# Attention's key-value products in four parts, one in front of each output tile of the last batch; query transposes gathered behind them

## The chip, the cores and the metric

The kernel runs on one core of a Trainium2 chip. The metric is device time in microseconds for one execution of the whole program. The engines are named as in the profile: PE (TensorE, matrix products and transposes), PEld (its weight loads), DVE (VectorE), ACT (ScalarE), POOL (GpSimd) and SP (SyncE, which issues DMAs).

## The reference, cut to what matters

Three stages follow each other: linear attention with a norm per head, a layer of eight experts with one chosen per token, and a gated layer. The change touches only the first.

```python
def _attn_ref(q, k, v, g_norm):          # 8 batches, 8 heads, 576 rows, 64 columns
    kv = np.einsum('bhsd,bhse->bhde', k, v)
    out = np.einsum('bhsd,bhde->bhse', q, kv)
    rms = np.sqrt(np.mean(out * out, axis=-1, keepdims=True) + 1e-06)
    return (out / rms * g_norm).astype(np.float32)
...
x = attn_out.transpose(0, 2, 1, 3).reshape(B * S, H * D)
x = _moe_ref(x=x, **moe_kwargs)          # logits, argmax, two products per expert
return _moe2_ref(x=x, **moe2_kwargs)     # (sigmoid(x @ w_gate) * (x @ w_val)) @ w_out
```

## The kernel before

The order of the instructions on each engine is the order in which the program emits them; no scheduler moves them. Each engine and each DMA queue works its own list in order and waits where an operand or a buffer isn't ready.

The attention stage is a loop over nine rounds, b = 0 to 8. Round b makes the key-value product of batch b and the outputs of batch b - 1. Inside, r runs from 0 to 4 over tiles of 128 query rows; the fifth tile of a pair of batches is shared, so only rounds with an even b make an output for r = 4, and only rounds with an odd b transpose a fifth query tile.

- emit_kv(b) does 72 products of 64x64 on PE (four pairs of heads c, nine row groups, two heads): the tile kv in PSUM. In the trace each fp32 product appears as two weight loads and two products, so 144 of each. Two DVE copies (L263, L264) put kv into R, block diagonal, in SBUF.
- emit_RT(b) transposes R on PE (L271, tile rtp), and DVE copies it to SBUF (L273). emit_M(b) multiplies it with the routing weights on PE (L279, tile mp), and DVE copies the 16 columns per pair back into R (L280).
- emit_qT transposes one query tile on PE (L285, tile qps); ACT copies it out (L287).
- emit_out(b - 1, r) is one output tile: products on PE (L299, tile ops), a copy and a square on ACT (L301, L304), a sum of squares on DVE (L305, into ssq).
- norm(b - 2), called at r = 1, is a chain of eight DVE operations (L314 to L328) with one ACT square root in it. rank (L349 to L368, even b from 4 on, at r = 1), lanes (L375, r = 3) and choose (odd b, r = 3) are routing steps, mostly on DVE.
- load_kv(b + 2) and load_q(b + 2) issue the loads on SP at r = 1. Keys and values have two buffers each, so the loads of batch b + 2 wait until emit_kv(b) has read its own.

In the kernel before, all of emit_kv(b) stands at the head of the round, and then each r has one output tile and one transpose of queries. PSUM has two buffers each for kv, rtp and mp together, for qps, and for ops.

Behind the attention comes a chain of small DVE steps that sort the tokens by expert, and then the two expert products and the gated layer, both long rows of matrix products.

Of the kernel before, what the change touches and what calls it, by code (L numbers as in the profile page):

```python
# [9 lines left out]
F32 = mybir.dt.float32  # L10
# [10 lines left out]
B, H, S, D = 8, 8, 576, 64  # L21
# [61 lines left out]
def attention_moe_glu_kernel(  # L83
# [4 lines left out]
    nc = tc.nc  # L88
# [70 lines left out]
    with ExitStack() as st:  # L159
# [3 lines left out]
        pkv = st.enter_context(tc.tile_pool(name="a_pkv", bufs=2, space=PSUM))  # L163
# [27 lines left out]
        Rs = [big.tile([128, 4, 144], F32, name=f"R{i}") for i in range(3)]  # L191

        q_t, k_t, v_t, qr_t = {}, {}, {}, {}

        def load_kv(b):

            if b < B:
                for src, dst, nm in ((k, k_t, "kt"), (v, v_t, "vt")):
                    t = dst[b] = ld.tile([128, 4, 9, D], F32, tag=nm, name=nm)
                    eng = nc.scalar if b == 0 and src is v else nc.sync  # L200
                    eng.dma_start(out=t.rearrange("p c r d -> p c (r d)"), in_=src[b].rearrange("(c i) (p r) d -> (i p) c (r d)", i=2, r=9))

        def load_q(b):

            if b < B:
                q_t[b] = ld.tile([128, H, 4, D], F32, tag="qt", name="qt")
                nc.sync.dma_start(out=q_t[b], in_=q[b, :, 0:512, :].rearrange("h (p r) d -> p h r d", r=4))
                if b % 2 == 0:
                    qr_t[b // 2] = ld.tile([128, H, D], F32, tag="qr", name="qr")
                half = slice(64 * (b % 2), 64 * (b % 2) + 64)  # L210
                nc.sync.dma_start(out=qr_t[b // 2][half], in_=q[b, :, 512:576, :].rearrange("h p d -> p h d"))
# [38 lines left out]
                    op=ALU.mult)  # L250
            nc.vector.tensor_tensor(out=bias, in0=bias, in1=lg, op=ALU.add)

        qT, o_t, me_t = {}, {}, {}

        def emit_kv(b):
            kv = pkv.tile([128, 4, 64], F32, tag="kv", name="kv")
            kt, vt, R = k_t.pop(b), v_t.pop(b), Rs[b % 3]
            for c in range(4):
                for r in range(9):
                    for i in range(2):  # L260
                        rows = slice(64 * i, 64 * i + 64)
                        nc.tensor.matmul(out=kv[rows, c, :], lhsT=kt[rows, c, r, :], rhs=vt[rows, c, r, :], start=(r == 0), stop=(r == 8))
            nc.vector.tensor_copy(out=R[0:64, :, 0:64], in_=kv[0:64])  # L263
            nc.vector.tensor_copy(out=R[64:128, :, 64:128], in_=kv[64:128])  # L264

# [9 lines left out]
        def emit_M(b):  # L275
            rt = mps_t.pop(b)
            ps = pkv.tile([128, 4, 128], F32, tag="kv", name="mp")
            for hp in range(4):
                nc.tensor.matmul(out=ps[:, hp, 0:16], lhsT=rt[:, hp, :], rhs=wpt[:, hp, :], start=True, stop=True)  # L279
            nc.vector.tensor_copy(out=Rs[b % 3][:, :, 128:144], in_=ps[:, :, 0:16])  # L280

        def emit_qT(key, src):
            ps = pq.tile([128, 4, 128], F32, tag="q", name="qps")
            for hp in range(4):
                nc.tensor.transpose(out=ps[:, hp, :], in_=src[:, hp * 128:hp * 128 + 128], identity=ident)  # L285
            t = wk.tile([128, 4, 128], F32, tag="qT", name="qT", bufs=5)
            nc.scalar.activation(out=t, in_=ps, func=ACTF.Copy)  # L287
            qT[key] = t
# [18 lines left out]
        def norm(b):  # L307

            r0, n = 4 * (b % 2), 4 + b % 2
            t0 = 9 * (b // 2) + r0  # L310
            rt, tt = (sm.tile([128, 72], F32, tag=z, name=z) for z in ("rt", "tt"))
            w, v = slice(8 * t0, 8 * t0 + 8 * n), slice(0, 8 * n)
            ms, rs, t = ssq[:, w], rsq[:, w], tt[:, v]
            nc.vector.tensor_scalar(out=ms, in0=ms, scalar1=1.0 / D, scalar2=1e-6, op0=ALU.mult, op1=ALU.add)  # L314
            nc.scalar.activation(out=rt[:, v], in_=ms, func=ACTF.Sqrt)
            nc.vector.reciprocal(out=rs, in_=rt[:, v])
            nc.vector.tensor_tensor(out=t, in0=rs, in1=rs, op=ALU.mult)
            nc.vector.scalar_tensor_tensor(out=t, in0=t, scalar=-0.5, in1=ms, op0=ALU.mult, op1=ALU.mult)
            nc.vector.scalar_tensor_tensor(out=rs, in0=t, scalar=1.5, in1=rs, op0=ALU.add, op1=ALU.mult)
            rs = rs.rearrange("p (n s) -> p n s", s=2)  # L320
            xo = o_t[b].rearrange("p n (c f) -> p (n c) f", f=144)
            u = uo[:, r0:r0 + n, :]
            nc.vector.tensor_tensor(out=u.rearrange("p n (c s e) -> p (n c) s e", c=4, s=2), in0=xo[:, :, 128:144].rearrange("p n (s e) -> p n s e", s=2),
                                    in1=rs.unsqueeze(3).broadcast_to([128, 4 * n, 2, 8]), op=ALU.mult)
            nc.gpsimd.tensor_copy(out=xo[:, :, 128:130], in_=rs)
            l = lg[:, t0:t0 + n, :]
            nc.vector.tensor_reduce(out=l, in_=u.rearrange("p n (h e) -> p n e h", e=8), op=ALU.add, axis=AX)
            nc.vector.tensor_tensor(out=l, in0=l, in1=bias[:, t0:t0 + n, :], op=ALU.add)  # L328
# [68 lines left out]
        for b in range(B + 1):  # L397
            if b < B:
                qc = wk.tile([128, 4, H, D], F32, tag="qc", name="qc", bufs=1)
                nc.scalar.activation(out=qc[:, 0], in_=q_t[b][:, :, 0, :], func=ACTF.Copy)  # L400
                emit_kv(b)
            if b == 2:
                make_bias()
            for r in range(5):
                if b == B and r == 0:
                    ld_scope.close()
                    mw = [mw_scope.enter_context(tc.tile_pool(name="m_wr0", bufs=1, side="right", reuse_waits="tile"))]
                    w1p = w1_scope.enter_context(tc.tile_pool(name="m_w1", bufs=3, side="right", reuse_waits="tile"))
                    half0 = mw[0].tile([128, 2, KC * F1], F32, tag="half0", name="half0")
                    w1r = [half0[:, 0].rearrange("p (c f) -> p c f", f=F1)]  # L410
                    w2r = [half0[:, 1].rearrange("p (c f) -> p c f", f=DM)]
                    nc.sync.dma_start(out=w1r[0], in_=w1[0].rearrange("(c p) f -> p c f", p=128))
                if b < B and r == 0:
                    nc.scalar.activation(out=qc[:, 1], in_=q_t[b][:, :, 1, :], func=ACTF.Copy)
                    for i in (2, 3):
                        nc.gpsimd.tensor_copy(out=qc[:, i], in_=q_t[b][:, :, i, :])
                if b:
                    emit_out(b - 1, r)
                if b < B:
                    if r == 0:  # L420
                        emit_RT(b)
                    if r < 4:
                        emit_qT((b, r), qc[:, r].rearrange("p h d -> p (h d)"))
                    elif b % 2:
                        emit_qT((b, 4), qr_t[b // 2].rearrange("p h d -> p (h d)"))
                    if r == 2:
                        emit_M(b)
                if r == 1:
                    load_kv(b + 2)
                    load_q(b + 2)  # L430
                    if b == 0:
                        load_mod()
                    if b > 1:
                        norm(b - 2)
                    for i in {6: (0, 1, 2), 7: (3, 4)}.get(b, ()):
                        store_x(i)
                if b % 2 and b > 1:
                    if r == 3:
                        choose(b // 2 - 1)
                elif b > 2:  # L440
                    if r == 1:
                        lane = rank(b // 2 - 2)
                    elif r == 3:
                        lo = lanes(b // 2 - 2, lane)
                        if b < B:
                            numbers(b // 2 - 2, lo, False)
# [59 lines left out]
        for t0 in range(0, NTILE, 9):  # L506
# [3 lines left out]
            for t in range(t0, t0 + 9):  # L510
                for w in range(2):
                    nc.tensor.matmul(out=ph[w][:, 0:NSLOT], lhsT=lid[:, t, w, :], rhs=soh[:, t, :],
                                     start=(t == 0), stop=(t == NTILE - 1))
# [38 lines left out]
    rows = [y0p.tile([128, 4, 256], F32, name=f"rows{i}") for i in range(2)]  # L552
# [27 lines left out]
    def turn(src, ps):  # L580

        for c in range(KC):
            nc.tensor.transpose(out=ps[:, c, :], in_=src[:, c * 128:c * 128 + 128], identity=ident)  # L583
# [416 lines left out]
    with ExitStack() as st:  # L1000
# [182 lines left out]
        for i in range(2 * HT):  # L1183
            p = i // 2
# [147 lines left out]
```

## Time and profile before

| | |
|---|---|
| median of 3 runs | 1486.94 us |
| all runs | 1486.31, 1494.65, 1486.94 us |
| profiled execution, its own time | 1496.44 us |
| its span | 1494.7 us |
| PE, PEld busy | 1429.6 us (96%), 1225.2 us (82%) |
| DVE, ACT, POOL busy | 909.2 us (61%), 638.9 us (43%), 228.6 us (15%) |
| mean granted PE clock | 0.984 |

The span runs from the first to the last instruction of the profiled execution; its own time holds 1.7 us more around it. The durations below come from that execution, which took 9.5 us longer than the median of the three runs. Attention takes about the first 133 us of the span, the sorting of tokens goes on until 161 us, and the rest is expert and gated layers.

### The profile page before, as it was taken

What the parts mean: (1) busy time and instruction counts of PE and PEld (TensorE: products, weight loads), DVE (VectorE), ACT (ScalarE), POOL (GpSimd) and SP (SyncE); (2) the same over time, 40 slices, a digit from 0 to 9 for tenths busy, and PEclk for the clock granted to TensorE, in tenths of its full rate; (3) what the DMA queues carried; (4) which work ended last, traced back from release to release, by engine and by line L of the source; (5) the groups of instructions that cost most, each with busy time, mean ns of one, the idle gap of its engine ahead of it and who ended that gap; (6) DMA issues with size and microseconds to landing.
All of it is one profiled execution on the core that took longest, in us unless ns stands there. A gap on an engine that the chain in (4) does not pass through costs nothing.

```text
span 1494.7 us, 22909 instructions
## 1 busy us (share of the span) xinstructions
PE 1429.6 (96%) x8633; PEld 1225.2 (82%) x8633; DVE 909.2 (61%) x1402; ACT 638.9 (43%) x1005; POOL 228.6 (15%) x302
## 2 busy tenths in 40 slices
PE   6984799999999999999999999999999999999997
PEld 6974689999999998778888887888888888888886
DVE  2557778788888877647876676343653436444442
ACT  3656455555555556746433342232322323221221
POOL 1011222222222221311011101010010200101011
PEclk9998799999999999999999999999999999999999
DMA  9975798858886766859886666556474564646444
GB/s 297 345 288 211 215 267 289 276 173 276 293 286 208 241 194 207 295 190 351 321 336 246 247 239 232 212 194 249 156 260 185 217 227 173 242 167 236 176 159 157
DMA packets 154979, 356.31 MB, mean 238 GB/s; under 512 B 20592, under 2 KB 74096, under 8 KB 147696
## 3 DMA queue, kind: packets, MB, share of 16 engines
q1 hardware_dynamic: 141872, 317.03, 61.0%
q0 software_dynamic: 11488, 36.27, 7.1%
q8 instruction: 71, 1.16, 0.3%
q10 hardware_dynamic: 1504, 1.48, 0.3%
q14 instruction: 44, 0.36, 0.1%
HBM read 311.27 MB, written 68.63 MB: 254 GB/s over the span
## 4 chain that ended last, share of the span: by engine, by line
PE 55%; DMA 1%; issue 0%; DVE 0%; POOL 0%; ACT 0%; POOLq 0%
PE gv L646 10%; PE gv L648 10%; PE gv L647 10%; PE ac L1163 6%; PE ac L1161 6%; PE ac L1162 6%; PE gv L620 1%; PE gv L621 1%; PE gv L622 1%; PE tr L583 1%; DMA wt_d<-wt 1%; POOL out_dram L1145 0%; DVE u L650 0%; POOLq L1328 0%; DVE wt L609 0%
## 5 line engine op out<-in xcount | busy, mean ns | idle before, releaser
L650 DVE TENSOR_TENSOR gm<-u,gv 128x512 f32<-128x512 f32 x96 | 65.9, 687 | 173.5 <-PE gv L648 172.3
L1161 PE MATMUL ac<-wos,gh 128*128 128x512 f32 x432 | 168.7, 390 | 0.0
L1163 PE MATMUL ac<-wos,gl 128*128 128x512 f32 x432 | 168.6, 390 | 0.0
L1162 PE MATMUL ac<-wos,gh 128*128 128x512 f32 x432 | 168.1, 389 | 0.0
L788 PE MATMUL ph<-xh,w1h 128*128 128x256 f32 x576 | 166.8, 290 | 0.8 <-ACT xh L771 0.8
L789 PE MATMUL ph<-xh,w1l 128*128 128x256 f32 x576 | 164.0, 285 | 1.2 <-DVE w1l L750 1.2
L790 PE MATMUL ph<-xl,w1h 128*128 128x256 f32 x576 | 164.1, 285 | 0.0
L670 ACT ACTIVATE s<-gv 128x512 f32<-128x512 f32 x48 | 28.8, 600 | 265.2 <-issue 207.7
L835 PE MATMUL py<-w2h,hh 128*128 128x512 f32 x304 | 119.3, 392 | 0.0
L836 PE MATMUL py<-w2l,hh 128*128 128x512 f32 x304 | 119.3, 392 | 0.0
L837 PE MATMUL py<-w2h,hl 128*128 128x512 f32 x304 | 118.5, 390 | 0.0
L646 PE MATMUL gv<-half,wt 128*128 128x512 f32 x288 | 113.3, 394 | 0.6 <-DVE u L650 0.6
L789 PEld LDWEIGHTS ph<-xh,w1l 128*128 128x128 f32 x576 | 111.3, 193 | 2.7 <-DVE w1l L750 1.4
L788 PEld LDWEIGHTS ph<-xh,w1h 128*128 128x128 f32 x576 | 111.2, 193 | 2.5 <-ACT xh L771 1.2
L648 PE MATMUL gv<-half,wt 128*128 128x512 f32 x288 | 112.5, 390 | 0.0
L647 PE MATMUL gv<-half,wt 128*128 128x512 f32 x288 | 112.1, 389 | 0.0
L790 PEld LDWEIGHTS ph<-xl,w1h 128*128 128x128 f32 x576 | 111.1, 193 | 0.3 <-DVE xl L772 0.3
L650 DVE TENSOR_TENSOR s<-u,gv 128x512 f32<-128x512 f32 x48 | 33.0, 688 | 118.3 <-PE gv L648 118.2
L1145 POOL DMA_INDIRECT out_dram<-ot,to x36 | 37.1, 1029 | 439.1 <-DVE ot L1142 190.4
L1163 PEld LDWEIGHTS ac<-wos,gl 128*128 128x128 f32 x432 | 81.1, 188 | 17.9 <-DVE gl L1130 0.4
L1162 PEld LDWEIGHTS ac<-wos,gh 128*128 128x128 f32 x432 | 81.1, 188 | 17.2
L1161 PEld LDWEIGHTS ac<-wos,gh 128*128 128x128 f32 x432 | 81.1, 188 | 17.0 <-ACT gh L1129 0.2
(275 smaller groups left out, 3323.7 us busy)
## 6 DMA issues: line engine op xcount, KB each, us to landing
wt<-wt_d SPq DMA_DIRECT2D x36, 1536.0 KB
wos<-wo_d SPq DMA_DIRECT2D x96, 512.0 KB
half<-in_moe_w_dram SPq DMA_DIRECT2D x88, 512.0 KB
w1r<-in_moe_w_dram SPq DMA_DIRECT2D x44, 512.0 KB
w2r<-in_moe_w_dram SPq DMA_DIRECT2D x44, 512.0 KB
rows<-w_d SPq DMA_DIRECT2D x24, 512.0 KB
wt<-wt_d SPq DMA_DIRECT2D x48, 256.0 KB
wt_d<-wt SPq DMA_DIRECT2D x12, 1024.0 KB
```

Source lines behind the costliest of these rows:

```text
L646: nc.tensor.matmul(out=o, lhsT=wh, rhs=yh[:, c, :], start=first and c == 0, stop=False, skip_group_check=True)
L647: nc.tensor.matmul(out=o, lhsT=wh, rhs=yl[:, c, :], start=False, stop=False, skip_group_check=True)
L648: nc.tensor.matmul(out=o, lhsT=wl, rhs=yh[:, c, :], start=False, stop=last and c == 1, skip_group_check=True)
L788: nc.tensor.matmul(out=o, lhsT=bh[:, c, cs], rhs=hi[:, c, 0:n], start=(c == 0), stop=False)
L789: nc.tensor.matmul(out=o, lhsT=bl[:, c, cs], rhs=hi[:, c, 0:n], start=False, stop=False)
L790: nc.tensor.matmul(out=o, lhsT=bh[:, c, cs], rhs=lo[:, c, 0:n], start=False, stop=(c == KC - 1))
L835: nc.tensor.matmul(out=o, lhsT=hi[:, f, cs], rhs=bh[:, f, :], start=first, stop=False)
L836: nc.tensor.matmul(out=o, lhsT=hi[:, f, cs], rhs=bl[:, f, :], start=False, stop=False)
L837: nc.tensor.matmul(out=o, lhsT=lo[:, f, cs], rhs=bh[:, f, :], start=False, stop=last)
L1161: nc.tensor.matmul(out=o, lhsT=gh[:, cs], rhs=wh, start=(k == 0), stop=False)
L1162: nc.tensor.matmul(out=o, lhsT=gh[:, cs], rhs=wl, start=False, stop=False)
L1163: nc.tensor.matmul(out=o, lhsT=gl[:, cs], rhs=wh, start=False, stop=(k == NJ - 1))
```

## The change

emit_kv now does one pair of heads c per call, and round b calls it for c = r in front of each output tile r = 0 to 3. After the fourth part a new function keep_kv makes the two DVE copies into R. The query transposes leave their places: the first and that of R come at r = 3 behind the output tile, the others at r = 4, with emit_M between the third and the fourth. The loads of keys and values are issued at r = 3, behind those of the queries, which stay at r = 1. load_mod and store_x move from r = 1 to r = 3. No computation is added or dropped.

```diff
+        def emit_kv(b, c):
+            if c == 0:
+                kv_t[b] = pkv.tile([128, 4, 64], F32, tag="kv", name="kv")
+            kv, kt, vt = kv_t[b], k_t[b], v_t[b]
+            for r in range(9):
...
+        def keep_kv(b):
+            kv, R = kv_t.pop(b), Rs[b % 3]
             nc.vector.tensor_copy(out=R[0:64, :, 0:64], in_=kv[0:64])
             nc.vector.tensor_copy(out=R[64:128, :, 64:128], in_=kv[64:128])
...
-                emit_kv(b)
...
+                if b < B and r < 4:
+                    emit_kv(b, r)
+                    if r == 3:
+                        keep_kv(b)
+                        load_kv(b + 2)
                 if b:
                     emit_out(b - 1, r)
                 if b < B:
-                    if r == 0:
+                    turn = lambda i: emit_qT((b, i), qc[:, i].rearrange("p h d -> p (h d)"))
+                    if r == 3:
+                        turn(0)
                         emit_RT(b)
-                    if r < 4:
-                        emit_qT((b, r), qc[:, r].rearrange("p h d -> p (h d)"))
-                    elif b % 2:
-                        emit_qT((b, 4), qr_t[b // 2].rearrange("p h d -> p (h d)"))
-                    if r == 2:
+                    if r == 4:
+                        turn(1)
+                        turn(2)
                         emit_M(b)
+                        turn(3)
+                        if b % 2:
+                            emit_qT((b, 4), qr_t[b // 2].rearrange("p h d -> p (h d)"))
                 if r == 1:
-                    load_kv(b + 2)
                     load_q(b + 2)
+                    if b > 1:
+                        norm(b - 2)
+                if r == 3:
                     if b == 0:
                         load_mod()
-                    if b > 1:
-                        norm(b - 2)
                     for i in {6: (0, 1, 2), 7: (3, 4)}.get(b, ()):
                         store_x(i)
```

Three places show what moves. The names are those of the section before; R2_146 is the R of batch 2, R0_144 that of batch 3, the number behind a name tells one tile from the next, and line numbers of the changed kernel are larger by 3 for the same statement.

On PE, round 3 before:

```order
L262 MATMUL kv_686<-vt_438,kt_436 64x64 x72
L299 MATMUL ops_765<-R2_146,qT_595 128x144 x4
L271 MATMUL rtp_774<-ident_65,R0_144 128x128 x4
L285 MATMUL qps_781<-ident_65,qc_684 128x128 x4
L299 MATMUL ops_788<-R2_146,qT_611 128x144 x4
L285 MATMUL qps_797<-ident_65,qc_684 128x128 x4
L299 MATMUL ops_823<-R2_146,qT_647 128x144 x4
L285 MATMUL qps_832<-ident_65,qc_684 128x128 x4
L279 MATMUL mp_839<-wpt_132,rt_779 128x16 x4
L299 MATMUL ops_845<-R2_146,qT_669 128x144 x4
```

On PE, round 3 of the changed kernel, from the third output tile on (ahead of it stand three parts of 18 products, with an output tile behind each of the first two):

```order
L302 MATMUL ops_778<-R2_146,qT_669 128x144 x4
L262 MATMUL kv_689<-vt_429,kt_427 64x64 x18
L302 MATMUL ops_811<-R2_146,qT_682 128x144 x4
L288 MATMUL qps_820<-ident_65,qc_684 128x128 x4
L274 MATMUL rtp_827<-ident_65,R0_144 128x128 x4
L288 MATMUL qps_841<-ident_65,qc_684 128x128 x4
L288 MATMUL qps_848<-ident_65,qc_684 128x128 x4
L282 MATMUL mp_855<-wpt_132,rt_832 128x16 x4
L288 MATMUL qps_861<-ident_65,qc_684 128x128 x4
L288 MATMUL qps_868<-ident_65,qr_226 128x128 x4
```

The 72 products are spread over the four output tiles, and the transpose of R stands behind all of them, one query transpose after the last output tile.

On DVE, the head of round 3 before:

```order
L263 COPY R0_144<-kv_686 64x4x64
L264 COPY R0_144<-kv_686 64x4x64
L305 TENSOR_REDUCE ssq_124<-sq_771 128x8
L273 COPY rt_779<-rtp_774 128x512
L305 TENSOR_REDUCE ssq_124<-sq_794 128x8
L314 TENSOR_SCALAR ssq_124<-ssq_124 128x40
```

On DVE, the head of round 3 of the changed kernel:

```order
L308 TENSOR_REDUCE ssq_124<-sq_715 128x8
L308 TENSOR_REDUCE ssq_124<-sq_742 128x8
L317 TENSOR_SCALAR ssq_124<-ssq_124 128x40
L319 RECIPROCAL rsq_125<-rt_748 128x40
L320 TENSOR_TENSOR tt_749<-rsq_125 128x40
L321 SCALAR_TENSOR_TENSOR tt_749<-tt_749,ssq_124 128x40
L322 SCALAR_TENSOR_TENSOR rsq_125<-tt_749,rsq_125 128x40
L326 TENSOR_TENSOR uo_126<-o_517,rsq_125 128x320
L330 TENSOR_REDUCE lg_138<-uo_126 128x40
L331 TENSOR_TENSOR lg_138<-lg_138,bias_134 128x40
L308 TENSOR_REDUCE ssq_124<-sq_784 128x8
L266 COPY R0_144<-kv_689 64x4x64
```

The copies into R (the second, L267, follows the last row shown), first in the round before, now stand behind three sums of squares and the whole norm of batch 1; in rounds 4 and 6 the ten operations of rank stand ahead of them as well.

On SP, the first loads inside the loop (round 0) before:

```order
L201 DMA kt<-in_k_dram 128x4x576
L201 DMA vt<-in_v_dram 128x4x576
L207 DMA qt<-in_q_dram 128x8x256
L211 DMA qr<-in_q_dram 64x8x64
L235 DMA mb<-in_moe_modality_bias_dram 128x16
```

and in the changed kernel:

```order
L207 DMA qt<-in_q_dram 128x8x256
L211 DMA qr<-in_q_dram 64x8x64
L201 DMA kt<-in_k_dram 128x4x576
L201 DMA vt<-in_v_dram 128x4x576
L235 DMA mb<-in_moe_modality_bias_dram 128x16
```

Queries go first in every round; nothing else changes place on this queue.

## Rows read from the trace of the kernel before

**Rows 1.** Waits of PE, 0 to 135 us: total us, times, longest us.

```profile
PE kv L262 <- DMA vt<-in_v_dram: 11.5, 2, 9.7
PE kv L262 <- issue: 9.0, 4, 3.4
PE ops L299 <- DVE R L280: 1.1, 1, 1.1
```

**Rows 2.** Timeline of PE, round 3: start, us, instruction [idle before <-releaser].

```profile
53.93 0.73 PE L262 MATMUL kv<-vt,kt 64*64 64x64 f32 x17 [1.70 <-issue]
54.59 1.25 PE L299 MATMUL ops<-R,qT 128*128 128x144 f32 x8
55.68 0.60 PE L271 MATMUL rtp<-ident,R 128*128 128x128 f32 x4
56.12 0.60 PE L285 MATMUL qps<-ident,qc 128*128 128x128 f32 x4
56.55 1.15 PE L299 MATMUL ops<-R,qT 128*128 128x144 f32 x8
```

**Rows 3.** Timeline, round 4: an undisturbed key-value product and the next output tile.

```profile
62.46 4.42 PE L262 MATMUL kv<-vt,kt 64*64 64x64 f32 x144
...
66.80 1.25 PE L299 MATMUL ops<-R,qT 128*128 128x144 f32 x8
```

**Rows 4.** Timeline of PE, the other pauses of rounds 5 to 8.

```profile
81.30 3.75 PE L262 MATMUL kv<-vt,kt 64*64 64x64 f32 x77 [3.16 <-issue]
...
99.82 1.15 PE L262 MATMUL kv<-vt,kt 64*64 64x64 f32 x31 [3.43 <-issue]
...
116.57 0.45 PE L262 MATMUL kv<-vt,kt 64*64 64x64 f32 x8 [0.75 <-issue]
...
125.95 2.23 PE L299 MATMUL ops<-R,qT 128*128 128x144 f32 x16 [1.06 <-DVE R L280]
```

**Rows 5.** Stretches: length, each engine's busy us (x instructions), PEclk, DMA share, GB/s.

```profile
53.90:78.20 24.30, 24.00 (x378) 22.71 (x379) 16.19 (x48) 17.26 (x32) 1.57 (x4) 1.00 1.05 337
81.20:96.40 15.20, 15.07 (x254) 14.46 (x253) 7.83 (x21) 8.61 (x16) 4.70 (x7) 0.90 0.71 237
...
80.80:84.20 3.40, 2.90 (x55) 2.89 (x56) 0.00 (x0) 0.00 (x0) 3.40 (x4) 0.51 0.02 5
...
101.30:104.70 3.40, 3.40 (x17) 3.39 (x17) 1.05 (x3) 1.43 (x3) 0.00 (x0) 0.50 1.01 412
```

**Rows 6.** DMA queues, 68.5 to 78.0 us, then 78.0 to 79.9: packets, MB, share.

```profile
q1 hardware_dynamic: 2386, 3.43, 102.5%
...
q8 instruction: 1, 0.02, 5.5%
```

**Rows 7.** Timeline of DVE, round 3: copy into R, sums of squares, norm.

```profile
54.70 0.42 DVE L263 COPY R<-kv 64x256 f32<-64x256 f32 x1 [2.96 <-PE kv L262]
...
59.08 0.69 DVE L305 TENSOR_REDUCE ssq<-sq 128x8 f32<-128x512 f32 x1 [0.45 <-ACT sq L304]
59.69 0.17 DVE L314 TENSOR_SCALAR ssq<-ssq 128x40 f32<-128x40 f32 x1
...
62.73 0.68 DVE L305 TENSOR_REDUCE ssq<-sq 128x8 f32<-128x512 f32 x1
...
63.45 0.68 DVE L305 TENSOR_REDUCE ssq<-sq 128x8 f32<-128x512 f32 x1
```

**Rows 8.** Timeline of DVE, round 4: norm, rank, next sum of squares.

```profile
71.96 0.17 DVE L314 TENSOR_SCALAR ssq<-ssq 128x32 f32<-128x32 f32 x1
...
74.72 0.28 DVE L349 TENSOR_REDUCE tr<-oh 128x8 f32<-128x72 bf16 x1
...
76.50 0.68 DVE L305 TENSOR_REDUCE ssq<-sq 128x8 f32<-128x512 f32 x1
```

**Rows 9.** Waits of PE, 170 to 1495 us, longest and last of eight.

```profile
PE tr L583 <- ACT yr L578: 2.1, 1, 2.1
...
PE gv L620 <- PEq L995: 0.3, 1, 0.3
```

More of the change, by code (lines that the diff above doesn't have):

```diff
@@ L251, in make_bias @@
             nc.vector.tensor_tensor(out=bias, in0=bias, in1=lg, op=ALU.add)
[L253 to L262, printed above, removed]
+        qT, o_t, me_t, kv_t = {}, {}, {}, {}
+        def emit_kv(b, c):
[3 more added lines that the diff above has]
+            for r in range(9):
+                for i in range(2):
+                    rows = slice(64 * i, 64 * i + 64)
+                    nc.tensor.matmul(out=kv[rows, c, :], lhsT=kt[rows, c, r, :], rhs=vt[rows, c, r, :], start=(r == 0), stop=(r == 8))
+        def keep_kv(b):
+            kv, R = kv_t.pop(b), Rs[b % 3]
             nc.vector.tensor_copy(out=R[0:64, :, 0:64], in_=kv[0:64])
```

## The prediction

> **What bounds the kernel now.** I read three views. The busy shares say that PE holds the program, so the list of what PE waits for comes next. Behind 170 us it shows eight pauses, 6.7 us together [rows 9], in work that the change doesn't touch. Up to 135 us there are more, and three of them matter: 11.5 us for the first loads of values, 9.0 us in four pauses inside the key-value products where nothing that the profile shows was missing ("issue"), and 1.1 us for R [rows 1].
>
> The timeline of PE says where the four are: with 17, 77, 31 and 8 of the 144 products of batches 3, 5, 6 and 7 still to run [rows 2, 4]. They lie at no boundary of the program. Between the end of one pause and the next PE ran 378 + 379 = 757 recorded instructions in one case and 254 + 253 = 507 in another [rows 5], close to 3 and 2 times 256; and a packet of the instruction queue, 0.02 MB, landed between 78.0 and 79.9 us, in the pause that ends at 81.30, while none did in the 9.5 us before, when the data queue kept the DMA engines at 102% [rows 6]. I read them as waits for the next block of instructions. A key-value product runs its 288 instructions in 4.34 us [rows 3], faster than anything around it, so it uses up a block before the next has come through the busy queues. After the two long pauses PE's granted clock was down at 1.2 GHz (0.50) for 3.4 us [rows 5].
>
> The Trainium skill, page "Runtime: NRT & Kernel Launch", section "Instruction fetch mechanics", has the same 16 KiB block of 256 instructions, but says that PE's instruction memory holds 2048 of them and that crossing a block is "mostly hidden". The trace agrees on the block and not on the rest: four crossings cost 9.0 us.
>
> **The change part by part.** All times of a round count from the start of its first key-value part.
>
> *Spreading the products: a gain.* Between two parts now lies an output tile of 16 instructions that takes 1.09 us [rows 2], against 72 in a part of 4.34 / 4 = 1.09 us [rows 3]. A block of 256 now lasts at least 256 / 88 x 2.18 = 6.3 us where it lasted 3.9, and I expect the pauses to go. What they cost in this execution: 1.70 + 3.16 + 3.43 + 0.75 = 9.04 us [rows 2, 4], and at half clock about half of 2.90 + 3.40 us busy, 3.15 [rows 5]. Batch 7's columns of R, for which PE waited 1.06 us at 125.95 [rows 4], are now finished behind the round's other DVE work with a transpose still to run, so that goes too. **Gain 13.2 us.** It is bounded by 0 (if the blocks still come late) and 13.2.
>
> *The copies into R: a loss.* Before, DVE made them as soon as the product was there, and PE had an output tile to do meanwhile (1.09 us, against 55.68 - 54.70 = 0.98 from first copy to the transpose of R) [rows 2, 7]. Now PE reaches the transpose of R after four parts, four output tiles and one query transpose: 4 x 1.09 + 4 x 1.09 + 0.43 = 9.15 us. DVE's list reaches the copies later. The second output tile starts at 1.09 + 1.09 + 1.09 = 3.27. Its sum of squares starts 59.08 - 56.55 = 2.53 later, the norm 0.61 behind that, the third sum 62.73 - 59.69 = 3.04 behind that, the first copy 0.72 later, the transpose of R 0.98 later [rows 2, 7]: 3.27 + 2.53 + 0.61 + 3.04 + 0.72 + 0.98 = 11.15. PE waits 2.0 us in rounds 3, 5 and 7. In rounds 4 and 6 norm and rank together take 76.50 - 71.96 = 4.54 instead of 3.04 [rows 8]: 12.65, a wait of 3.5. Round 2 has the smaller norm, 74.72 - 71.96 = 2.76 [rows 8], and no rank: 10.87, 1.7. Round 1 has no norm: the third sum follows its own output tile, at 5.45 + 2.53, and the transpose 1.70 later, 9.68: 0.5. **Loss 3 x 2.0 + 2 x 3.5 + 1.7 + 0.5 = 15.2 us.** All of it stands on PE, which has nothing to do in between: all later transposes are queued behind that of R. Least it could be a third less, if ACT and DVE deliver the sums earlier than where a query transpose's copy stood ahead of them; at most 3 us more, if M then waits for the copy of R's transpose as well.
>
> *Edits I cost at nothing.* Query transposes run back to back at 0.43 to 0.44 us [rows 2] as before; their copies on ACT hide under M and the next part, and if they don't, the upper bound above holds that. The loads of keys and values wait on SP until the fourth part is done, some 4 us later, with the queries ahead of them; they are needed two rounds on, more than 20 us later, and PE waited for values in two rounds only, 11.5 us of which 9.7 is the start [rows 1]. Round 2 could pay the other 1.8 us once more; I take 0 and keep 1.8. store_x and load_mod have still a round or more until they are read. POOL's list is unchanged.
>
> *The sum.* Against the profiled execution of 1496.44 us: + 15.2 - 13.2 = + 2.0 us. The median is 9.5 us below that execution. Behind 170 us the pauses are 6.7 us in all [rows 9], too little to hold the difference, while the four pauses and the half clock behind them are 12.2 us and depend on how busy the queues are. So I take about two thirds of the 9.5, 6.3 us, to be pauses that the median run doesn't have and can't win back. The loss is the program's order and is the same in each run: 1486.94 + 2.0 + 6.3 = **1495 us**.
>
> **The rivals.**
>
> *The exchange comes out on the winning side.* The blocks cost the median run what they cost the profiled one, and the wait for R is half of what I have: 1486.94 - 13.2 + 7.6 = 1481 us. For it: the pauses are measured and the wait is put together from pieces of another order. Against it: norm and rank stand ahead of the copies in DVE's list. It decides at a mean wait of 13.2 / 7 = 1.9 us in front of the transpose of R: below that the change wins.
>
> *The new pauses bring half clock.* A pause of 3.16 and one of 3.43 us were followed by 3.4 us at 0.50, one of 1.70 was not [rows 2, 4, 5]. Five pauses of 2.0 to 3.5 us could each cost 3.4 / 2 = 1.7 us more: 1495 + 8.5 = 1503.5 us.
>
> *There was nothing to win.* If fetching blocks costs the median run nothing, the loss stands alone: 1486.94 + 15.2 = 1502 us. That is what the skill's page says of fetching. For it is that the four executions shown differ by up to 10.1 us for no reason that the profile names; against it, that the four pauses sit at multiples of 256 instructions.
>
> *The pauses stay.* If the blocks come late in the spread order too, only the 1.1 us at 125.95 is won: 1486.94 + 15.2 - 1.1 = 1501 us at most, less where a pause falls in front of the wait for R and hides in it. That lies inside my forecast's range.
>
> **How the numbers follow.** Forecast, 1490 to 1501: 0.55. Winning exchange, 1474 to 1487: 0.17, with 0.05 more for a gain beyond it. Half clock: 0.12. Nothing to win: 0.11. The range reaches down into the winning exchange and up over the two slow rivals: 1482 to 1505 us. One per cent, about what a measurement of this kernel can tell from no change, is 14.9 us: faster is below 1472, slower above 1501.8. Slower gets most of the two last rivals, 0.20; faster 0.06; the rest, 0.74, is within 1%.
>
> **What would show it.** Right: no "issue" pause longer than 1 us inside the key-value products; instead a pause of PE in front of the transpose of R in rounds 2 to 7, ended by DVE's copies, larger in rounds 4 and 6, 15 us in all. DVE's copies start behind norm. Wrong: if that wait is under 1 us each, the DVE term fails and the kernel is faster; if "issue" pauses remain, the reading of the blocks fails; if the granted clock falls inside attention more than twice, the third rival holds.

## The result, and the profile after

| | before | after |
|---|---|---|
| median (lowest to highest) of 6 runs each | 1487.38 us (1485.07 to 1494.65) | 1505.08 us (1502.49 to 1507.57) |
| profiled execution, span | 1496.44, 1494.7 us | 1502.89, 1501.1 us |
| PE, DVE, ACT busy | 1429.6, 909.2, 638.9 us | 1436.4, 910.6, 641.9 us |
| mean granted PE clock | 0.984 | 0.985 |

The ratio is 1.0107 [1.0078, 1.0135]: slower by about 16 us. The two profiled executions are only 6.4 us apart, the medians 17.7; what lies between them is a point of its own below.

The waits of PE after the change (total us, times, longest us, 0 to 150 us) answer to [rows 1]:

```profile
PE kv L262 <- DMA vt<-in_v_dram: 11.2, 2, 9.7
PE rtp L274 <- DVE R L267: 10.2, 7, 2.6
...
PE kv L262 <- issue: 0.7, 1, 0.7
...
```

The pauses inside the key-value products fell from 9.0 us to one of 0.7, batch 7's wait for R is gone, the wait for values is as it was, and a new line stands second: the transpose of R waits for DVE's copies, 10.2 us (9.8 in rounds 2 to 7, the rest in round 0). The timeline of PE, round 3 (start, us, instruction, [idle before <-releaser]), answers to [rows 2]:

```profile
53.42 1.26 PE L262 MATMUL kv<-vt,kt 64*64 64x64 f32 x36
54.61 1.25 PE L302 MATMUL ops<-R,qT 128*128 128x144 f32 x8
55.79 1.26 PE L262 MATMUL kv<-vt,kt 64*64 64x64 f32 x36
...
64.75 0.66 PE L274 MATMUL rtp<-ident,R 128*128 128x128 f32 x4 [1.34 <-DVE R L267]
...
68.11 1.26 PE L262 MATMUL kv<-vt,kt 64*64 64x64 f32 x36
...
80.94 0.65 PE L274 MATMUL rtp<-ident,R 128*128 128x128 f32 x4 [2.58 <-DVE R L267]
...
85.27 1.26 PE L262 MATMUL kv<-vt,kt 64*64 64x64 f32 x36
...
106.48 0.68 PE L262 MATMUL kv<-vt,kt 64*64 64x64 f32 x17 [0.73 <-issue]
...
131.74 2.13 PE L302 MATMUL ops<-R,qT 128*128 128x144 f32 x16
```

Count from the round's start, 53.42 and 68.11: the transpose of R runs at 11.33 us in round 3 and at 12.83 in round 4. A part and its tile last 55.79 - 53.42 = 2.37 us. The rounds last 14.69 and 17.16 us. Before, round 4 took 13.49 us, and round 3 began with the row below and ended at 62.46 [rows 3]: without its pause of 1.70 us, 12.47.

```profile
48.29 3.94 PE L262 MATMUL kv<-vt,kt 64*64 64x64 f32 x127
```

The last output tiles of attention start at 131.74 where they started at 125.95 [rows 4]: of the 6.4 us between the profiled executions, 5.8 had come about by then.

On DVE, round 4, the timeline shows what stands ahead of the copies; it answers to [rows 8]:

```profile
71.94 0.69 DVE L308 TENSOR_REDUCE ssq<-sq 128x8 f32<-128x512 f32 x1 [4.42 <-ACT sq L307]
74.31 0.69 DVE L308 TENSOR_REDUCE ssq<-sq 128x8 f32<-128x512 f32 x1 [1.68 <-ACT sq L307]
74.91 0.17 DVE L317 TENSOR_SCALAR ssq<-ssq 128x32 f32<-128x32 f32 x1
...
77.67 0.28 DVE L352 TENSOR_REDUCE tr<-oh 128x8 f32<-128x72 bf16 x1
...
79.44 0.68 DVE L308 TENSOR_REDUCE ssq<-sq 128x8 f32<-128x512 f32 x1
80.04 0.41 DVE L266 COPY R<-kv 64x256 f32<-64x256 f32 x1
80.46 0.43 DVE L267 COPY R<-kv 64x256 f32<-64x256 f32 x1
```

DVE waited for the second sum's input and then ran norm, rank and the third sum from 74.31 until 80.04, with a single wait of 0.30 us in between; only then came the copies, for a product that PE had finished before its fourth output tile.

Windows of the same trace (length, busy us and instructions of PE, PEld, DVE, ACT, POOL, granted clock, DMA share, GB/s):

```profile
21.50:24.90 3.40, 3.02 (x40) 2.94 (x41) 0.00 (x0) 0.00 (x0) 0.00 (x0) 0.50 1.13 284
60.00:90.00 30.00, 25.91 (x399) 23.30 (x398) 17.49 (x49) 17.49 (x31) 6.88 (x8) 1.00 0.61 202
676.80:680.20 3.40, 3.20 (x12) 2.91 (x13) 2.24 (x5) 3.36 (x7) 0.00 (x0) 0.51 1.05 310
```

The clock falls to half once in the rounds of attention, behind the start of the loads, and not behind the waits for R. One more such stretch lies at 676.8 us, in work that the change doesn't touch, behind a wait of 3.0 us for ACT that was 2.1 before [rows 9].

### The profile page after: what moved, and what is told of

It is laid out like the page before. It is cut to its first block, busy times and chain, and to the rows that moved or that the text cites. A ratio compares the mean times of both kernels' runs of the same rounds, so it can differ in the third digit from the quotient of the medians.

```text
span 1501.1 us, 22899 instructions
## 1 busy us (share of the span) xinstructions
PE 1436.4 (96%) x8633; PEld 1226.6 (82%) x8633; DVE 910.6 (61%) x1402; ACT 641.9 (43%) x1005; POOL 227.0 (15%) x302
## 4 chain that ended last, share of the span: by engine, by line
PE 54%; DMA 1%; issue 0%; DVE 0%; POOL 0%; ACT 0%; POOLq 0%
PE gv L656 10%; PE gv L658 10%; PE gv L657 10%; PE ac L1173 6%; PE ac L1171 6%; PE ac L1172 6%; PE gv L630 1%; PE gv L632 1%; PE gv L631 1%; PE tr L593 1%; DMA wt_d<-wt 1%; POOL out_dram L1155 0%; DVE u L660 0%; POOLq L1338 0%; DVE wt L619 0%
```

## The experiments

The theory going in: the gain is real where the pauses occur, but DVE's order makes the transpose of R wait (10.2 us), and changing between 64x64 products and 128-wide tiles costs something of its own. The rivals: the gathering of the transposes is what costs; or the split. A ratio is against runs of the kernel before beside the experiment.

**The kernel before once more**, profiled, to see whether the pauses belong to the program or to the execution. No edit.

> The kernel before, unchanged, for a second profiled execution. Theory A (the four pauses inside the key-value products belong to the profiled execution, whose queues are busier, and the timed median has next to none): pauses marked issue return, 5 to 10 us together, at the same instruction counts, and the profiled execution takes 1493 to 1498 us, well above the timed median of 1487. Theory B (the pauses were a chance of that one execution): under 3 us of them, and the profiled execution is within 3 us of the median.

It took 1490.91 us. The timeline of its PE at the pauses:

```profile
52.91 0.73 PE L262 MATMUL kv<-vt,kt 64*64 64x64 f32 x17 [2.23 <-issue]
...
96.11 1.97 PE L262 MATMUL kv<-vt,kt 64*64 64x64 f32 x31 [3.76 <-issue]
113.98 0.45 PE L262 MATMUL kv<-vt,kt 64*64 64x64 f32 x8 [0.73 <-issue]
```

and windows behind two of them, with the granted clock:

```profile
54.30:57.70 3.40, 3.40 (x18) 3.39 (x17) 1.34 (x3) 1.88 (x3) 0.00 (x0) 0.50 1.14 306
95.30:102.10 6.80, 5.99 (x49) 5.87 (x50) 1.27 (x3) 1.34 (x3) 0.00 (x0) 0.50 1.02 423
```

The same 17, 31 and 8 products are left as in [rows 2, 4]: the places belong to the program. The lengths do not: 6.7 us together instead of 9.0, that of batch 5 (3.16 us) is absent, and that of batch 3 (2.23, was 1.70) now has half clock behind it. My theory, that a profiled execution with such pauses takes well longer than the other runs, failed: this one is within 0.3 us of the median of the 13 runs beside it, 1490.7.

The packets of the instruction queue (the traces' DMA queues, read in windows of 0.1 us) say more than the counts did. In all traces of this case together, 14 pauses stand inside the key-value products, and each ended 2.2 to 3.2 us after such a packet; in between the packets come some 10 us apart. Batch 5's came at 78.1 us in the first profile, which has the pause, and at 73.5, ahead of the product, in the second, which hasn't. This supports that PE waits there for instructions; no experiment tests it directly.

**Gathering alone**: the whole product in front of the first output tile, the transposes behind the tiles as in the changed kernel.

```diff
-                if b < B and r < 4:
-                    emit_kv(b, r)
-                    if r == 3:
-                        keep_kv(b)
-                        load_kv(b + 2)
+                if b < B and r == 0:
+                    for c in range(4):
+                        emit_kv(b, c)
+                    keep_kv(b)
+                if b < B and r == 3:
+                    load_kv(b + 2)
```

> The whole key-value product is back at the head of the round with its two copies into R; the transposes stay gathered behind the output tiles and the queries load first. Theory A (the loss is the wait for R behind the norm plus the alternation of 64x64 and 128x128 work on PE): both are gone, no wait of PE for the copies into R, 1484 to 1491 us timed; the issue pauses come back in its profile. Rival (gathering the transposes or loading the queries first is what costs): 1497 us or more.

1521.23 us, ratio 1.0211 [1.0168, 1.0253]. I had expected it to win, and it is the slowest of all. PE's timeline in round 3, then two windows:

```profile
54.83 5.52 PE L262 MATMUL kv<-vt,kt 64*64 64x64 f32 x144
60.28 4.43 PE L302 MATMUL ops<-R,qT 128*128 128x144 f32 x32
...
68.19 0.63 PE L288 MATMUL qps<-ident,qc 128*128 128x128 f32 x4 [2.16 <-ACT qT L290]
69.79 1.06 PE L282 MATMUL mp<-wpt,rt 128*128 128x16 f32 x8 [0.98 <-DVE rt L276]
...
```
```profile
53.90:57.30 3.40, 3.40 (x51) 3.07 (x52) 0.22 (x1) 1.63 (x3) 1.16 (x2) 0.50 0.88 322
88.00:94.80 6.80, 6.18 (x76) 5.85 (x78) 2.65 (x4) 2.70 (x6) 4.88 (x4) 0.50 0.01 2
```

Four output tiles in a row outrun ACT, which copies and squares each; the gathered transposes then wait for ACT to copy their results (2.16 us here), M for DVE, and the clock is at half for a part of each round (0.80 to 0.93 on average in stretches of about a round). There is no wait for R and no pause inside the products. So the parts between the tiles do a second thing that I had not seen: they give ACT and DVE time.

**The split alone**: parts in front of the tiles, query transposes one behind each tile as before, that of R behind the fourth tile, M behind the fifth.

```diff
                     if r == 3:
-                        turn(0)
                         emit_RT(b)
-                    if r == 4:
-                        turn(1)
-                        turn(2)
+                    if r < 4:
+                        turn(r)
+                    else:
                         emit_M(b)
-                        turn(3)
```

> The key-value product in four parts as changed, but the query transposes back behind each output tile (r = 0 to 3), so that PE reaches the transpose of R three transposes (1.3 us) later. Theory A: the wait for R falls from 10.2 to about 2 to 3 us, but the product with the routing weights now follows soon and waits about 1 us a round for the copy of R's transpose, which stands behind a sum of squares on DVE: 1499 to 1505 us. Rival (gathering is the loss): 1487 to 1492 us.

1514.86 us, ratio 1.0176 [1.0133, 1.0219]. Its waits of PE, 20 to 140 us:

```profile
PE rtp L274 <- DVE R L267: 9.4, 7, 2.2
PE mp L282 <- DVE rt L276: 4.6, 5, 1.7
```

I had expected the wait for R to fall to 2 to 3 us and the time to 1499 to 1505. In rounds 2 to 7 the wait is 8.5 us, against 9.8 with the whole change: a transpose between two tiles also puts off the next tile and so its sum on DVE (R's transpose runs at 11.98 us of round 3). With one transpose left to run between that of R and M instead of two, M waits for DVE's copy as well. And the clock fell to half twice, behind a wait of 1.68 us for rt and one of 2.06 us for R, both for DVE:

```profile
41.20:44.60 3.40, 3.40 (x42) 3.19 (x42) 1.38 (x4) 1.63 (x3) 0.00 (x0) 0.53 1.05 364
119.40:122.80 3.40, 3.40 (x24) 2.68 (x23) 2.01 (x3) 1.13 (x2) 1.28 (x1) 0.52 1.03 426
```

Each half of the change alone is worse than both together: the gathered transposes cover M's wait, and the parts cover ACT's.

**Norm and rank behind the copies into R.** The sum of squares of the fourth output tile goes behind the copy of R's transpose; else the changed kernel.

```diff
-            nc.vector.tensor_reduce(out=ssq[:, 8 * t:8 * t + 8], in_=sq, op=ALU.add, axis=AX)
+            summed = lambda: nc.vector.tensor_reduce(out=ssq[:, 8 * t:8 * t + 8], in_=sq, op=ALU.add, axis=AX)
+            if r != 3 or b == B - 1:
+                summed()
+            return summed
...
                         emit_RT(b)
+                        if b:
+                            summed()
...
                 if r == 1:
                     load_q(b + 2)
-                    if b > 1:
+                    if b == B:
                         norm(b - 2)
...
+                if r == 4 and 1 < b < B:
+                    norm(b - 2)
```

(choose and rank with what follows them move behind norm.)

> The changed kernel, but in rounds 2 to 7 the norm, choose, rank and lanes come at the end of the round, and the sum of squares of the fourth output tile comes behind the copy of R's transpose. Parts, transposes and loads stay as changed. Theory A: the waits of PE for R and for rt, 10.4 us together in the changed kernel, fall under 2 us, and the alternation cost (about 5 us) stays: 1494 to 1498 us. Rival (the alternation and the gathered transposes are the whole loss and PE would have waited for something else): 1502 us or more.

1494.94 us, ratio 1.0042 [1.0019, 1.0065]. The wait for R is gone from rounds 1 to 7, and the time fell by 1.0107 - 1.0042 = 0.65%, 9.7 us (8.4 between the profiled executions), for a wait of 10.2. The list of waits, 30 to 120 us, and the starts of rounds 3 and 4:

```profile
PE qps L288 <- ACT qT L290: 1.6, 6, 0.4
PE kv L262 <- DMA vt<-in_v_dram: 1.2, 1, 1.2
```
```profile
53.40 1.26 PE L262 MATMUL kv<-vt,kt 64*64 64x64 f32 x36
...
67.21 1.26 PE L262 MATMUL kv<-vt,kt 64*64 64x64 f32 x36
```

So DVE's order is shown to be the cause of that wait. But a round still takes 67.21 - 53.40 = 13.81 us here, against 12.47 before, with 0.37 us of waits in it: the split itself costs.

**How often PE changes tiles.** Two kernels, each the last one with another number of pieces: two halves, in front of the first and third output tile; and eight pieces, with a second one in the middle of each tile (keep_kv then comes behind the fourth tile).

```diff
-                if b < B and r < 4:
+                if b < B and r in (0, 2):
                     emit_kv(b, r)
+                    emit_kv(b, r + 1)
...
```
```diff
...
+                    emit_kv(b, r, range(5))
+                    second = lambda: emit_kv(b, r, range(5, 9))
...
+                if hp == 2 and middle is not None:
+                    middle()
```

> The kernel with norm at the end of the round, but the product in two halves, in front of the first and the third output tile. Alternation theory (each change between the 64x64 products and the 128-wide ones and back costs PE about 0.2 us): two fewer pairs of changes in seven rounds, 2.8 us less than with four parts, about 1492 us. Rival (the parts cost nothing, they only give ACT time): 1495 us or more, with PE waiting more for ACT.

> The kernel with norm at the end of the round, but the product in eight parts, one in front of and one in the middle of each of the four output tiles: twice the alternations, nothing else moved. Alternation theory: four more pairs of changes in seven rounds, 28 x 0.2 = 5.6 us more, about 1500.5 us, all of it in the time from one round to the next on PE. Rival (alternating is free and the longer rounds come from waits): 1494 to 1496 us.

1490.81 us, 1.0008 [0.9983, 1.0032], with two pieces; 1503.73 us, 1.0075 [1.005, 1.01], with eight; 1494.94 with four. Round 3 on PE, with two and then with eight:

```profile
50.23 2.31 PE L262 MATMUL kv<-vt,kt 64*64 64x64 f32 x72
52.48 2.23 PE L302 MATMUL ops<-R,qT 128*128 128x144 f32 x16
54.63 1.43 PE L262 MATMUL kv<-vt,kt 64*64 64x64 f32 x41
56.37 1.14 PE L262 MATMUL kv<-vt,kt 64*64 64x64 f32 x31 [0.31 <-issue]
```
```profile
54.32 0.80 PE L262 MATMUL kv<-vt,kt 64*64 64x64 f32 x20
55.05 0.76 PE L304 MATMUL ops<-R,qT 128*128 128x144 f32 x4
55.74 0.68 PE L262 MATMUL kv<-vt,kt 64*64 64x64 f32 x16
56.35 0.76 PE L304 MATMUL ops<-R,qT 128*128 128x144 f32 x4
57.04 0.80 PE L262 MATMUL kv<-vt,kt 64*64 64x64 f32 x20
```

The same work, 36 products and a tile, takes (54.63 - 50.23) / 2 = 2.20 us in halves, 2.37 in quarters, 57.04 - 54.32 = 2.72 in eighths. With a fixed price c for one piece and its return, halves and quarters give c = 2 x (2.37 - 2.20) = 0.34, quarters and eighths 2.72 - 2.37 = 0.35, where I had expected about 0.2. By the medians it is 4.1 us for 7 x 2 more changes (0.29 each) and 8.8 for 7 x 4 (0.31); by the ratios 5.1 and 4.9 us (0.36 and 0.18), uncertain by some 5 us each. So the times of the whole program bear out the direction, and the price rests on the rows. A rival for the quarters' cost, more waits, fails: there are none between these rows.

**The whole product late**, in front of the fourth tile of the changed kernel: one change a round, and nothing of the split.

```diff
-                if b < B and r < 4:
-                    emit_kv(b, r)
-                    if r == 3:
-                        keep_kv(b)
-                        load_kv(b + 2)
+                if b < B and r == 3:
+                    for c in range(4):
+                        emit_kv(b, c)
+                    keep_kv(b)
+                    load_kv(b + 2)
```

> The changed kernel, but all four parts of the product stand together in front of the fourth output tile; transposes gathered and norm early as changed. Theory C (in the run with the whole product at the head, PE ran out of work because ACT was still copying and squaring four output tiles when it should have copied out the transposes, and the pauses brought half clock): here the product itself, 4.3 us, gives ACT the time, and norm runs earlier too, so PE waits for ACT and for R under 6 us together up to 135 us and there is no half clock in the rounds: 1490 to 1499 us. Rival (gathering the transposes costs by itself, wherever the product stands): 1512 us or more.

1500.86 us, 1.0072 [1.0047, 1.0096], just above the 1490 to 1499 that I expected. PE's waits, 20 to 140 us, and a row of ACT in round 1:

```profile
PE ops L302 <- ACT o L304: 7.5, 5, 5.7
PE kv L262 <- issue: 3.0, 2, 2.0
...
```
```profile
25.89 0.63 ACT L403 ACTIVATE qc<-qt 128x512 f32<-128x512 f32 x1 [5.34 <-DMA qt<-in_q_dram]
```

The wait of 5.7 us for ACT is one of the start: in round 1 PE now comes to the third tile before the queries of the next batch have landed, and ACT, which stands waiting for them, can't copy the tiles. Between 30 and 120 us the tiles wait 0.9 us for ACT. The pauses inside the products are back (3.0 us), and half clock with them (0.50 from 65.0 to 68.4 us, behind the one of 1.98), which I had not expected. The wait for R is down to 1.3 us, although norm stands ahead of the copies: PE arrives later.

**Halves, with the transposes back between the tiles.** Norm and routing stay at the end of the round. First with halves in front of the first two tiles, the transpose of R behind the second tile, M behind the fourth and norm after the fifth; then the same with the waits that this left taken away: R's transpose one tile later, M behind the fifth, and the numbering of tokens (POOL) moved to the next round, behind POOL's copies of the queries.

```diff
-                if b < B and r < 4:
-                    emit_kv(b, r)
+                if b < B and r < 2:
+                    emit_kv(b, 2 * r)
+                    emit_kv(b, 2 * r + 1)
...
+                    if r == 1:
                         emit_RT(b)
+                    if r < 4:
+                        turn(r)
...
+                    if r == 3:
                         emit_M(b)
```
```diff
...
+                    if late:
+                        numbers(*late.pop(), False)
...
-                    if r == 1:
+                    if r == 2:
                         emit_RT(b)
...
-                    if r == 3:
+                    if r == 4:
                         emit_M(b)
...
-                        numbers(b // 2 - 2, lo, False)
+                        late.append((b // 2 - 2, lo))
```

> A version meant to beat both: the product in two halves in front of the first two output tiles, one transpose of queries behind each output tile as in the kernel before, the transpose of R behind the second tile, the routing product behind the fourth, norm and routing at the end of the round. Theory: one more pair of changes a round than before costs 1.4 us, no wait for R or ACT over 0.5 us, and the shorter bursts lose less to the fetch of instruction blocks (under 4 us of issue pauses): 1484 to 1489 us, level with the kernel before or a little below. Rival (a wait for the copy of R or of its transpose comes back): 1495 us or more.

> The version with two halves in front of the first two output tiles, with what was left in its trace taken away: the transpose of R moves behind the third output tile (it waited 1.5 us for R behind norm and rank in even rounds), the routing product to the end of the round, and POOL multiplies the token numbers behind its copies of the queries instead of ahead of them (PE waited 1.4 us for those copies, twice). Theory: PE waits under 1 us for R, rt and POOL together between 30 and 120 us, 6 us less than that version: 1483 to 1488 us, faster than the kernel before by 0.1 to 0.5%. Rival (the waits only move to ACT or to the routing at the end of attention): 1489 to 1492 us, no difference.

The first: 1490.66 us, 1.0005 [0.9983, 1.0027], above the 1484 to 1489 that I expected. The second: 1486.33 us, **0.9973 [0.9953, 0.9993]**, by the ratio about 4 us faster than the kernel before, with an interval that ends just below 1, and some 20 faster than the change. Waits of PE, 30 to 120 us, of the first and of the second:

```profile
PE rtp L274 <- DVE R L267: 3.1, 2, 1.7
PE qps L288 <- POOL qc L419: 2.8, 2, 1.4
PE kv L262 <- issue: 0.2, 1, 0.2
```
```profile
PE mp L282 <- DVE rt L276: 1.1, 4, 0.3
PE ops L302 <- DVE R L283: 0.3, 1, 0.3
PE kv L262 <- issue: 0.2, 1, 0.2
```

Two pieces are enough to do away with nearly all pauses, and the first transpose of the experts starts at 151.8 us in the second, where the two profiles of the kernel before have 160.9 and 158.3.

## Why the prediction came out as it did

The sign of the sum was right and its size too small: 1495 forecast, 1505.08 measured, at the upper end of the range; slower by over 1%, to which I gave 0.20, is what happened (1.07% by the ratio, from 0.78% on by its interval).

*The gain was right where the pauses are.* 9.04 us became 0.73, batch 7's 1.06 us went, and there is no half clock in those rounds: 8.3 + 1.06 + 3.15 = 12.5 us, forecast 13.2. That spreading is what does it fits all kernels that split the products (0 to 1.1 us of pauses in attention). The gathered kernel has none with all 144 in one piece; there PE is held up so long elsewhere that blocks may have come in time, which is a reading and not shown. What the pauses wait for is still inferred, from counts and packets.

*DVE's side of the wait for R was right.* The transpose runs at 11.33 us of odd rounds and 12.83 of even ones, forecast 11.15 and 12.65; moving norm gave back 9.7 us. Round 2 was off (11.53, forecast 10.87), and round 1 had no wait for R where I had 0.5.

*PE's side was mis-sized, and that is the step that failed.* "4 x 1.09 + 4 x 1.09 + 0.43 = 9.15 us" took each piece's length from a row in which it stood among other work. A part and a tile last 2.37 us and not 2.18, so PE is ready for R at 64.75 - 1.34 - 53.42 = 9.99. The wait comes out smaller, 9.8 us in rounds 2 to 7 and not 14.7; but PE spends that time on its own work. Attention's last tiles start 5.8 us later, so the loss is 5.8 + 12.5 = 18.3 us where I had 15.2: 9.8 for R; by the price of the rows, 7 x 3 more changes at 0.34 to 0.35 us, 7.1 to 7.4 for changing; and 1.1 to 1.4 that I leave as smaller gaps. The first cut of the product is taken at the price of the later ones there. What I had costed at nothing, the alternating of parts and tiles, is the term left out.

*The third rival did not happen* in the profiled execution: none of its waits for R, up to 2.58 us, was followed by half clock. With the split alone two waits for DVE were, so the rival isn't excluded in kind; but over whole runs it finds little room: the six runs after have a median granted clock of 0.985, the 60 of the kernel before beside the experiments one between 0.985 and 0.986. *The rival of nothing to win* comes near the time: with the loss as measured it gives 1486.94 + 18.3 = 1505.2 us. Its cause, that the pauses cost an ordinary run nothing, is hard to hold: the second profile has 6.7 us of them in an execution that lies within 0.3 us of the median of the 13 runs beside it, 1490.7. If the pauses are fetches, the Trainium skill's page "Runtime: NRT & Kernel Launch", section "Instruction fetch mechanics", by which crossing a block is mostly hidden, is right on most crossings, and my prediction read too much into four: by an estimate from that page's block, PE's 8633 + 8633 = 17266 recorded instructions are some 67 blocks of 256, and the four pauses stand at four of them. On how many instructions PE holds, no trace here says anything.

*From the profiled 6.4 to the timed 17.7 us.* I had added 6.3 for pauses that the median run doesn't have. Part of the rest is the six runs of the kernel before: their median is 1487.38 us, those beside the experiments 1490.7, 1489.75 and 1492.38 (13, 30 and 17 runs). Against its second profile, 1490.91, the profiled execution after takes 12.0 us more, and lies itself 2.2 under the median after: 14.2 us, against 16 by the ratio. Of the 12.0, 8.3 lie ahead of the first transpose of the experts (158.3 and 166.6 us) and 3.7 behind it, where no instruction was changed; the two profiles of the kernel before differ there by 3 us too. Of the 8.3, 1.4 are the half clock behind the start of the loads, which that second profile doesn't have: round 1's first part and tile take 3.72 us instead of 2.37. Of the 3.7, 3.3 lie at one wait for ACT, that at 676.8 us: from its start to the fifth product of 512 columns behind it PE takes 6.4 us, with a wait of 3.03 and half clock, and 3.1 us in that second profile, with a wait of 1.10 and full clock. Why ACT was later stays open. That the pauses' lengths make the runs spread fits, but isn't shown: 30 runs of the kernel before lie 16.4 us apart, 9 runs with eight pieces 3.3. The granted clock does go with the time: of those 60 runs, the 14 at a clock of 0.982 or 0.983 have a median of 1494.5 us, the 19 at 0.987 or more one of 1485.8.

## What to carry to other kernels

Before moving a producer later on one engine, read the list of the engine that takes its result: here the copy came behind norm and rank, in an order written for the old place, and 10.2 us of waiting followed. A duration read between two neighbours holds for those neighbours; price each change between kinds of tiles by itself, and split a run of small products no further than the pauses need. Do both halves of a change apart before crediting either: here each alone was worse than the two.

## What the runs showed of the hardware

- One change from 64x64 fp32 products to 128-wide output products and back cost 0.34 to 0.35 us by the rows, between two, four and eight pieces; the times of the whole program are too uncertain to price it.
- The pauses inside the products keep their places and not their lengths: 17, 31 and 8 products from the end in both executions, with 1.70, 3.43, 0.75 us and 2.23, 3.76, 0.73 us. Each of 14 ended 2.2 to 3.2 us after a packet of the instruction queue.
- Half clock followed issue pauses of 1.98 (the whole product late), 2.23, 3.16, 3.43 and 3.76 us, waits for DVE of 1.68 and 2.06 us (the split alone) and one for ACT of 3.03 us (the change). It followed neither an issue pause of 1.70 nor, in the changed kernel, waits for R of 1.34 to 2.58 us. So neither the length of a wait nor what is waited for tells by itself whether it follows.
